# Performer attention and two feed-forward layers on one core: which queue positions the splits and sums take, and which engine adds the weight sums

## Chip, cores and metric

One core of one Trainium2 chip runs the whole program. The metric is the device time of one execution in microseconds (us); lower is better.

## What is computed

```python
def reference(**kwargs):
    ...
    attn_out = _attn_ref(**attn_kwargs)          # random-feature attention: 4 batches, 8 heads, 576 positions, 64 wide, 128 features
    x = np.ascontiguousarray(attn_out.transpose(0, 2, 1, 3)).reshape(B * S, H * D)   # 2304 x 512
    x = _moe_ref(x=x, **moe_kwargs)              # h = x @ w_in; (h * clip(h + 3, 0, 6) / 6) @ w_out, d_ff = 2048
    return _moe2_ref(x=x, **moe2_kwargs)         # h = x @ w_in; (h * sigmoid(1.702 h)) @ w_out
```

## The kernel before

All matrix products run in a split form: an fp32 operand becomes a high part (a ScalarE copy that rounds) and a low part (a VectorE subtract), and three products hi·hi, hi·lo, lo·hi are accumulated. Of each batch's 576 positions 512 form a block; the 64 left over of all four batches form one block of 256.

The first layer (to 578 us) goes over units (n, c): batch n, chunk c of 16 chunks of d_ff. `emit_h` multiplies a chunk (L501) and makes its gated, split activation (L512, L513, L517, L518; the last two are put into `gate`); `emit_o`, two units later, multiplies it with the output weights (L551). In between, a callback `side()`, called at two places of each, issues the attention of the next batch in small steps and, at every second call, one entry of the list `late`. `late` prepares the second layer's weights while batches 1 to 3 run: `convert_1` and `convert_2` rebuild them (GpSimd L195, VectorE L202), then `sums(u, n)` with n from 0 to 7 for each of 8 pairs of chunks u. `put_sums` copies a quarter pair with ScalarE (L218), subtracts with GpSimd (L219) and stores the result; `add_sums` (L231 to L234) replaces the quarters by sums and differences in place, four adds of 128x256 for each of the two weights.

The second layer multiplies 2x2 blocks with 7 products instead of 8, so it needs sums of blocks of x, of weights and of gated activations. It treats two batches at once, p = 0 and p = 1. `x_ops` makes the 14 split operands of x for one pair in 16 steps: twice (q = 0, 1) a load and seven parts, each a ScalarE copy (L637) and a VectorE subtract (L638), four of them with a GpSimd sum (L625 to L631). `h_pair` (L846) is called for u = 0 to 7 and gives the gated activations `gt[u, e]`; `o_pair` then runs the products 1, 7, 6, 5, 2, 3, 4, each over u = 0 to 7. I call one such u of one product a turn: 56 turns, 12 matmuls each (L965). For each turn `halves` splits one quarter of g into a ring of three `gs` buffers (ScalarE L939, VectorE L940), and `total` may add quarters in place on GpSimd for a later product (op 7 L955, op 6 L957, op 5 L959, op 4 L961). After each turn a callback `side()` issues steps of `x_ops` for the next pair, spread evenly.

Nothing here fixes the final order: the program is recorded in this order, and a scheduler then sets each engine's queue from data dependences, its own costs and the ties it is given. `tc.issue_after(ins)`, wrapped in `behind`, ties every instruction of a block behind `ins` if it is on the same engine; it is an order in the queue, not a wait. The queues are in order: an instruction that waits holds all behind it on its engine.

Of the kernel before, what the change touches and what calls it, by code (L numbers as in the profile page):

```python
# [1 line left out]

# [6 lines left out]
F32 = mybir.dt.float32  # L9
# [6 lines left out]
ALU = mybir.AluOpType  # L16
# [6 lines left out]
def performer_moe_kernel(  # L23
# [13 lines left out]
    nc = tc.nc  # L37
# [22 lines left out]
    PREP = 9  # L60
# [28 lines left out]
            return acc.tile(shape, F32, tag="acc", name="acc")  # L89
        return psp.tile(shape, F32, tag="ps", name="ps")  # L90

    def behind(i):
        return nullcontext() if i is None else tc.issue_after(i.ins)


    qkv = {}
# [130 lines left out]
    def add_sums(u, k):  # L227
        w0, w1 = whole[2 * u][:, k], whole[2 * u + 1][:, k]
        a11, a22 = w0[:, 0], w1[:, 1]
        a12, a21 = (w0[:, 1], w1[:, 0]) if k == 0 else (w1[:, 0], w0[:, 1])  # L230
        nc.vector.tensor_tensor(out=a22, in0=a21, in1=a22, op=ALU.add)  # L231
        nc.vector.tensor_tensor(out=a21, in0=a11, in1=a21, op=ALU.subtract)  # L232
        nc.vector.tensor_tensor(out=a11, in0=a22, in1=a11, op=ALU.subtract)
        nc.vector.tensor_tensor(out=a12, in0=a12, in1=a11, op=ALU.subtract)  # L234

    def sums(u, n):

# [516 lines left out]
    def side():  # L754
        pace[1] += 1
        if pace[1] % 2:
            late_at("side", 1)
            return
        while todo and (pace[0] - len(todo)) * 4 * NC < pace[0] * pace[1]:
            todo.pop()()  # L760
# [31 lines left out]
    for u in range(len(units) + LAG):  # L792
        while fetches and fetches[0][0] <= u + AHEAD:
            fetch_w(0, *fetches.pop(0)[1:])
        if u < len(units):
            n, c = units[u]
            if c == 0 and n + 1 < B:
                xblk[n + 1] = new_x(n + 1)
                steps = att_steps(Att(n + 1, xblk[n + 1], xl, n == 0))
                todo = steps[::-1]  # L800
                pace[:] = len(todo), 0
            if (n, c) == (B - 2, NC - 1):
                while todo:
                    todo.pop()()
                actx.close()
                lp = ctx.enter_context(
                    tc.tile_pool(name="lp", bufs=1, side="right", reuse_waits="tile")
                )
                xblk[B] = new_x(B)
                for kk in range(NK):  # L810
                    split_x(xl, xblk[B], kk)
            if n > 0:
                before_chunk(n, c)
            emit_h(n, c, side)
            if n == 0:
                convert_next(2, min(c + 2, NC), *(att.feat[H - 1] if c == 0 else ()))
            if n == B - 1 and c >= PREP:
                if c == PREP:
                    assert n_late[0] == len(late), (n_late, len(late))
                    prep = x_ops(0, wp, "w")  # L820
                    n_prep = len(prep)
                for _ in range(-(-n_prep // (NC - PREP))):
                    if prep:
                        prep.pop(0)()
            if c == NC - 1:
                while todo:
                    todo.pop()()
        if u >= LAG:
            emit_o(*units[u - LAG], side)
# [6 lines left out]
    def h_pair(p, u, first_split):  # L836

        psum, tag, oth, otag = (acc, "acc", psp, "ps") if u % 2 else (psp, "ps", acc, "acc")
        w = {}

        def product(op, kind, j, ps, first):
            s = w[kind][:, j].rearrange("p s (q f) -> p s q f", q=2)
            m = 0
            for q in range(2):
                for wi, xi in ((0, 0), (0, 1), (1, 0)):
                    nc.tensor.matmul(  # L846
                        out=ps,
                        lhsT=s[:, wi, q, :],
                        rhs=xop[q, op][:, xi],
                        start=(first and m == 0),  # L850
                        stop=(m == 5),
                        skip_group_check=not first,
                    )
                    m += 1

        def rest(e, ps):
            kinds = "ab"[e]
            m = 0
            for j in range(2):
                s = w[kinds][:, j].rearrange("p s (q f) -> p s q f", q=2)  # L860
                for q in range(2):
                    for wi, xi in ((0, 0), (0, 1), (1, 0)):
                        nc.tensor.matmul(  # L863
                            out=ps[:, e, :],
                            lhsT=s[:, wi, q, :],
                            rhs=xblk[B][:, xi, 2 * j + q, :],
                            start=(m == 0),
                            stop=(m == 11),
                        )
                        m += 1  # L870

        def bank():
            return psum.tile([P, SM], F32, tag=tag, name="h")

        def temp(pool, tag, name):
            return pool.tile([P, SM], F32, tag=tag, bufs=3, name=name)

        def add(out, a, b):
            nc.vector.tensor_tensor(out=out, in0=a, in1=b, op=ALU.add)  # L879

        def gated(i, src, eng):

            if i % 2 == 0 and (u, i // 2) not in gt:
                gt[u, i // 2] = l1.tile([P, 2, SM], F32, tag=f"g{2 * u + i // 2}", name="g")
            g = gt[u, i // 2][:, i % 2]
            nc.scalar.activation(out=g, in_=src, func=AF.Sigmoid, scale=1.702)  # L886
            eng.tensor_tensor(out=g, in0=g, in1=src, op=ALU.mult)  # L887

        last = p == B // 2 - 1
        w["a"] = next_item()  # L890
        b1, b6 = bank(), bank()
        product(1, "a", 0, b1, True)
        p1 = temp(gp, "ga", "p1")
        nc.scalar.copy(p1, b1)
        w["d"] = next_item()
        product(6, "d", 0, b6, True)
        u2 = temp(gp, "ga", "u2")
        add(u2, p1, b6)
        product(2, "a", 1, b1, False)
        gated(0, b1, nc.vector)  # L900
        if last:
            pl = oth.tile([P, 2, B * SL], F32, tag=otag, name="hl")
            rest(0, pl)
        w["c"] = next_item()
        b5, b7 = bank(), bank()
        product(5, "c", 1, b5, True)
        t = temp(gp, "ga", "t")
        add(t, u2, b5)
        product(7, "c", 0, b7, True)
        c22 = temp(lp, "gs", "c22")  # L910
        add(c22, t, b7)
        product(3, "d", 1, b5, False)
        c12 = temp(lp, "gs", "c12")
        add(c12, u2, b5)
        w["b"] = next_item()
        gated(2, c12, nc.gpsimd)
        gated(3, c22, nc.gpsimd)
        first_split()
        product(4, "b", 1, b7, False)
        c21 = temp(lp, "gs", "c21")  # L920
        add(c21, u2, b7)
        gated(1, c21, nc.gpsimd)
        if last:
            rest(1, pl)
            if u % 2 == 0:
                pool, tag = ((l1, "xr"), (xp_, "xl"), (l1, "gl"), (l1, "xr"))[u // 2]
                gl[u // 2] = pool.tile([P, 2, 2, B * SL], F32, tag=tag, bufs=2 if tag == "xr" else 1, name="gl")
            g = gl[u // 2][:, u % 2]
            nc.scalar.activation(out=g, in_=pl, func=AF.Sigmoid, scale=1.702)
            nc.vector.tensor_tensor(out=g, in0=g, in1=pl, op=ALU.mult)  # L930
# [2 lines left out]
    gl = {}  # L933

    ready = []

    def halves(pool, N, g):
        s = pool.tile([P, 2, N], F32R, tag="gs", bufs=3, name="gs")
        nc.scalar.copy(s[:, 0], g)  # L939
        nc.vector.tensor_tensor(out=s[:, 1], in0=g, in1=s[:, 0].bitcast(F32), op=ALU.subtract)  # L940
        return s

    def o_pair(p, side):
# [6 lines left out]

        def total(op, u):
            b11, b12, b21, b22 = quarters(u)
            add = nc.gpsimd.tensor_tensor
            if op == 7:
                add(out=b12, in0=b22, in1=b12, op=ALU.subtract)  # L955
            elif op == 6:
                add(out=b11, in0=b12, in1=b11, op=ALU.add)  # L957
            elif op == 5:
                add(out=b12, in0=b22, in1=b11, op=ALU.subtract)  # L959
            elif op == 4:  # L960
                add(out=b21, in0=b21, in1=b11, op=ALU.subtract)  # L961

        def rows(s, w, out, d, start, stop, fresh):
            for m, (wi, gi) in enumerate(((0, 0), (1, 0), (0, 1))):
# [8 lines left out]

        def product(op, ps, first):
            src = {1: 0, 7: 1, 6: 0, 5: 1, 2: 2, 3: 3, 4: 2}[op]
            ahead = {1: 7, 7: 6, 6: 5, 3: 4}.get(op)
            more = last and op in (2, 3, 4)
            for u in range(NC // 2):
                if u % 2 == 0:
# [88 lines left out]
    for p in range(B // 2):  # L1068
# [4 lines left out]
        if p + 1 < B // 2:  # L1073
            prep = x_ops(p + 1, l1, "xr") + [left_x]

        turn = [0, len(prep)]

        def side():
            turn[0] += 1
            while prep and (turn[0] - 6) * turn[1] > (turn[1] - len(prep)) * 48:  # L1080
                prep.pop(0)()

        o_pair(p, side)
        gt.clear()
# [58 lines left out]
```

## Time and profile before

| | before |
|---|---|
| median of 3 runs | 965.95 us (965.52 to 967.58) |
| the profiled execution | 966.03 us |
| its span, first to last instruction | 964.2 us |
| TensorE (PE) matmul busy | 922.5 us, 96% |
| VectorE (DVE) busy | 659.7 us, 68% |
| ScalarE (ACT) busy | 481.2 us, 50% |
| GpSimd (POOL) busy | 361.1 us, 37% |

The stages lie at 0 to 578 us (attention and first layer; the weights of the second are prepared from 200 to 500), 578 to 653 (`h_pair`, p = 0), 653 to 742 (`o_pair`, p = 0), 742 to 852 (`h_pair`, p = 1) and 852 to the end (`o_pair`, p = 1). A matmul's end is modelled, so a busy TensorE may still be short of its fastest pace; idle time of another engine costs nothing by itself. The granted TensorE clock is 1.00 throughout.

### The profile page before, as it was taken

To read this page: it belongs to the slowest core of one execution; us is meant where nothing else is said; L and a number is where in the kernel's file an instruction comes from. 1 tells how busy PE (TensorE), PEld (TensorE's weight loads), DVE (VectorE), ACT (ScalarE), POOL (GpSimd) and SP (SyncE) were. 2 spreads that over 40 slices of the span, in tenths; PEclk is the share of its full clock that TensorE was granted. 3 is DMA by queue.
4 is the path that set the end of the run, shared out by engine and by line. 5 is a ranking of instruction groups with operands and counts; after the bars stand their busy time and mean duration, and the time that the engine had idled before them with its cause. 6 is when DMAs were issued, how large, how long until landed. Compare 5 with 4: busy or idle time off the path is not lost.

```text
span 964.2 us, 16360 instructions
## 1 busy us (share of the span) xinstructions
PE 922.5 (96%) x6238; PEld 785.4 (81%) x6238; DVE 659.7 (68%) x1010; ACT 481.2 (50%) x977; POOL 361.1 (37%) x271
## 2 busy tenths in 40 slices
PE   8899999999999999999999999997799999999997
PEld 6777767778778777878888888886799888889997
DVE  7888889599686877847876244448976443378743
ACT  5887676566654665536544234334444232243443
POOL 0112222055352424425444005758822254364400
PEclk9999999999999999999999999999999999999999
DMA  6667778889777867756684237765567545555572
GB/s 195 226 233 247 243 255 267 294 293 351 263 269 283 311 244 277 249 206 240 241 292 166 93 134 257 232 206 189 158 178 237 181 169 175 168 176 165 173 259 88
DMA packets 71133, 214.06 MB, mean 222 GB/s; under 512 B 7056, under 2 KB 12816, under 8 KB 71056
## 3 DMA queue, kind: packets, MB, share of 16 engines
q1 hardware_dynamic: 70896, 212.77, 65.6%
q8 instruction: 49, 0.80, 0.3%
q10 hardware_dynamic: 160, 0.26, 0.1%
q14 instruction: 28, 0.23, 0.1%
HBM read 157.43 MB, written 55.57 MB: 221 GB/s over the span
## 4 chain that ended last, share of the span: by engine, by line
PE 48%; DVE 12%; ACT 3%; issue 2%; DMA 2%; POOL 1%; SPq 0%; DVEq 0%; POOLq 0%
PE o L965 16%; PE h L846 16%; PE o L551 6%; PE ps L501 5%; DVE gs L940 2%; PE hl L863 2%; DVE xo L638 2%; DMA xr<-xs 2%; DVE w L202 1%; DVE gs L518 1%; DVE w L231 1%; POOL w L195 1%; DVE ga L513 1%; DVE w L232 1%; PE ps L256 1%
## 5 line engine op out<-in xcount | busy, mean ns | idle before, releaser
L965 PE MATMUL o<-wss,gs 128*128 128x256 f32 x1536 | 190.9, 284 | 13.5 <-DVE gs L940 13.4
L965 PEld LDWEIGHTS o<-wss,gs 128*128 128x128 f32 x1536 | 186.3, 191 | 18.4 <-DVE gs L940 17.7
L501 PE MATMUL ps<-x,wss 128*128 128x512 f32 x768 | 194.0, 397 | 5.2 <-DVE ga L513 1.5
L501 PEld LDWEIGHTS ps<-x,wss 128*128 128x128 f32 x768 | 139.3, 188 | 38.0 <-ACT wss L205 3.0
L195 POOL TENSOR_TENSOR w<-w,wpow 128x512 f32<-128x512 f32 x64 | 78.2, 1241 | 235.8 <-DVE wpow L190 137.7
L846 PE MATMUL h<-xo,wss 128*128 128x512 f32 x672 | 160.6, 393 | 0.0
L940 DVE TENSOR_TENSOR gs<-g,gs 128x512 fp32r<-128x512 f32 x112 | 114.7, 1047 | 45.8 <-ACT gs L939 45.2
L846 PEld LDWEIGHTS h<-xo,wss 128*128 128x128 f32 x672 | 124.1, 188 | 26.4 <-issue 0.2
L219 POOL TENSOR_TENSOR wsn<-w,wsn 128x512 fp32r<-128x512 f32 x64 | 91.0, 1436 | 69.7 <-ACT wsn L218 63.4
L939 ACT CAST gs<-g 128x512 fp32r<-128x512 f32 x112 | 69.4, 620 | 95.4 <-PE o L965 90.1
L551 PE MATMUL o<-gs,wsh 128*128 128x512 f32 (+1 forms) x480 | 111.8, 377 | 1.2 <-DVE ob L580 1.0
L551 PE MATMUL o<-gs,wss 128*128 128x512 f32 (+1 forms) x480 | 109.6, 374 | 2.4 <-ACT gs L517 2.4
L887 POOL TENSOR_TENSOR g<-g,c 128x512 f32<-128x512 f32 x48 | 64.1, 1336 | 101.4 <-ACT g L886 100.9
L551 PEld LDWEIGHTS o<-gs,wss 128*128 128x128 f32 x480 | 81.7, 188 | 17.5 <-ACT gs L517 3.4
L551 PEld LDWEIGHTS o<-gs,wsh 128*128 128x128 f32 x480 | 81.7, 188 | 17.4 <-DVE ob L580 1.2
L513 DVE SCALAR_TENSOR_TENSOR ga<-ga,ps 128x512 f32<-128x512 f32 (+1 forms) x80 | 49.8, 627 | 59.4 <-ACT ga L512 59.0
L512 ACT ACTIVATE ga<-ps,three 128x512 f32<-128x512 f32 (+1 forms) x80 | 51.7, 653 | 67.9 <-PE ps L501 67.9
L264 ACT ACTIVATE e<-ps,mx 128x128 f32<-128x128 f32 x220 | 62.8, 394 | 31.7 <-DVE mx L262 31.5
L202 DVE TENSOR_TENSOR w<-w,wtop 128x512 f32<-128x512 f32 x64 | 68.1, 1073 | 12.5 <-POOL w L195 12.0
L518 DVE TENSOR_TENSOR gs<-ga,gs 128x512 fp32r<-128x512 f32 (+1 forms) x80 | 63.3, 802 | 13.3 <-ACT gs L517 11.9
L886 ACT ACTIVATE g<-c 128x512 f32<-128x512 f32 x48 | 30.3, 632 | 78.8 <-DVE c L879 78.8
L517 ACT CAST gs<-ga 128x512 fp32r<-128x512 f32 (+1 forms) x80 | 45.7, 581 | 30.9 <-DVE ga L513 30.7
(154 smaller groups left out, 1257.4 us busy)
## 6 DMA issues: line engine op xcount, KB each, us to landing
wss<-left SPq DMA_DIRECT2D x64, 512.0 KB, 3.7
wss<-ws0i SPq DMA_DIRECT2D x48, 512.0 KB, 4.8
wraw<-in_w_in_dram SPq DMA_DIRECT2D x32, 512.0 KB, 4.6
wraw<-in_w_out_dram SPq DMA_DIRECT2D x32, 512.0 KB, 5.9
left<-wsn SPq DMA_DIRECT2D x32, 512.0 KB, 4.8
wss<-ws0o SPq DMA_DIRECT2D x24, 512.0 KB, 4.9
ws0i<-wss SPq DMA_DIRECT2D x16, 512.0 KB, 3.1
wss<-sumsa SPq DMA_DIRECT2D x16, 512.0 KB, 3.2
```

What stands on the lines that cost most here:

```text
L195: nc.gpsimd.tensor_tensor(out=w[:, cols], in0=w[:, cols], in1=q[:, cols], op=ALU.mult)
L202: nc.vector.tensor_tensor(out=wj, in0=wj, in1=a[:, j * DM:(j + 1) * DM], op=ALU.add)
L219: nc.gpsimd.tensor_tensor(out=s[:, :, 1], in0=t, in1=s[:, :, 0].bitcast(F32), op=ALU.subtract)
L264: act = nc.scalar.activation(out=e[:, r, :], in_=ps[:, r, :], func=AF.Exp, bias=mx[:, r:r + 1])
L501: nc.tensor.matmul(out=ps, lhsT=w[:, wi, kk, :], rhs=x[:, xi, kk, :], start=(m == 0), stop=(m == 3 * NK - 1),)
L518: gate[1] = nc.vector.tensor_tensor(out=s[:, 1, :], in0=g, in1=s[:, 0, :].bitcast(F32), op=ALU.subtract)
L551: nc.tensor.matmul(out=ps[:, e, :], lhsT=w[:, wi, cols], rhs=s[:, gi, :], start=(c == 0 and m == 0 and per == 1), stop=(c == NC - 1 and m ...
L846: nc.tensor.matmul(out=ps, lhsT=s[:, wi, q, :], rhs=xop[q, op][:, xi], start=(first and m == 0), stop=(m == 5), skip_group_check=not first,)
L887: eng.tensor_tensor(out=g, in0=g, in1=src, op=ALU.mult)
L939: nc.scalar.copy(s[:, 0], g)
L940: nc.vector.tensor_tensor(out=s[:, 1], in0=g, in1=s[:, 0].bitcast(F32), op=ALU.subtract)
L965: nc.tensor.matmul(out=out, lhsT=s[:, gi, d * P:(d + 1) * P], rhs=w[:, wi, :], start=(start and m == 0), stop=(stop and m == 2), skip_grou ...
```

## The change

Five edits. `behind` takes several instructions. The adds of `add_sums` go from VectorE to GpSimd. In the first layer, the `late` entries that `side()` issues are tied behind `gate`, and the 16 `x_ops` steps of the first pair are issued by `side()`, one at every fourth call and tied too, instead of three per chunk. In `h_pair` the sum of op 7 is made on the spot, and `o_pair` makes the sums of ops 6, 5 and 4 in the phases of products 1, 6 and 2. In `o_pair`, the steps of `x_ops` are issued at the turns listed in `PLACES`, tied behind the newest split and sum.

```diff
-    def behind(i):
-        return nullcontext() if i is None else tc.issue_after(i.ins)
+    def behind(*ins):
+        stack = ExitStack()
+        for i in ins:
+            if i is not None:
+                stack.enter_context(tc.issue_after(i.ins))
+        return stack
...
-        nc.vector.tensor_tensor(out=a22, in0=a21, in1=a22, op=ALU.add)
-        nc.vector.tensor_tensor(out=a21, in0=a11, in1=a21, op=ALU.subtract)
-        nc.vector.tensor_tensor(out=a11, in0=a22, in1=a11, op=ALU.subtract)
-        nc.vector.tensor_tensor(out=a12, in0=a12, in1=a11, op=ALU.subtract)
+        nc.gpsimd.tensor_tensor(out=a22, in0=a21, in1=a22, op=ALU.add)
+        nc.gpsimd.tensor_tensor(out=a21, in0=a11, in1=a21, op=ALU.subtract)
+        nc.gpsimd.tensor_tensor(out=a11, in0=a22, in1=a11, op=ALU.subtract)
+        nc.gpsimd.tensor_tensor(out=a12, in0=a12, in1=a11, op=ALU.subtract)
...
         if pace[1] % 2:
-            late_at("side", 1)
+            with behind(*gate):
+                late_at("side", 1)
+                if prep and pace[1] % 4 == 1:
+                    prep.pop(0)()
             return
...
-            if n == B - 1 and c >= PREP:
-                if c == PREP:
-                    assert n_late[0] == len(late), (n_late, len(late))
-                    prep = x_ops(0, wp, "w")
-                    n_prep = len(prep)
-                for _ in range(-(-n_prep // (NC - PREP))):
-                    if prep:
-                        prep.pop(0)()
+            if (n, c) == (B - 1, PREP):
+                assert n_late[0] == len(late)
+                prep = x_ops(0, wp, "w")
...
         gated(1, c21, nc.gpsimd)
+        g = gt[u, 1]
+        nc.gpsimd.tensor_tensor(out=g[:, 0], in0=g[:, 1], in1=g[:, 0], op=ALU.subtract)
...
+    PLACES = (4, 10, 12, 14, 16, 26, 27, 28, 29, 30, 42, 44, 46, 48, 50, 52, 54)
+    split_ins = [None, None, None]
...
-        nc.scalar.copy(s[:, 0], g)
-        nc.vector.tensor_tensor(out=s[:, 1], in0=g, in1=s[:, 0].bitcast(F32), op=ALU.subtract)
+        split_ins[0] = nc.scalar.copy(s[:, 0], g)
+        split_ins[1] = nc.vector.tensor_tensor(
+            out=s[:, 1], in0=g, in1=s[:, 0].bitcast(F32), op=ALU.subtract
+        )
...
-            ahead = {1: 7, 7: 6, 6: 5, 3: 4}.get(op)
+            ahead = {1: 6, 6: 5, 2: 4}.get(op)
...
-        turn = [0, len(prep)]
+        turn = [0]
 
         def side():
             turn[0] += 1
-            while prep and (turn[0] - 6) * turn[1] > (turn[1] - len(prep)) * 48:
-                prep.pop(0)()
+            if prep and turn[0] in PLACES:
+                with behind(*split_ins):
+                    prep.pop(0)()
```

`total` keeps ops 6, 5 and 4 as a table (all now one line, L967) and stores its instruction in `split_ins[2]`. Lines after L92 shift: VectorE's split of g is L940 before and L947 now, its split of x L638 and L642, the sums of x L625 to L631 and L629 to L635.

What the scheduler makes of it is shown at three places, with the tile numbers that the build gives. The first is VectorE in the middle of the weight stretch (`w` are weights, `ga` and `gs` the activation and its split, `mx` a row maximum of the attention, `thi` and `tlo` a split of its input). Before:

```order
L231 TENSOR_TENSOR w_3207<-w_3207 128x256
L232 TENSOR_TENSOR w_3207<-w_3193,w_3207 128x256
L233 TENSOR_TENSOR w_3193<-w_3207,w_3193 128x256
L234 TENSOR_TENSOR w_3193<-w_3193 128x256
L513 SCALAR_TENSOR_TENSOR ga_3365<-ga_3365,ps_3348 128x512
L518 TENSOR_TENSOR gs_3368<-ga_3365,gs_3368 128x512
L231 TENSOR_TENSOR w_3207<-w_3193,w_3207 128x256
L232 TENSOR_TENSOR w_3193<-w_3193 128x256
L262 TENSOR_REDUCE mx_3427<-ps_3419 128x4
L233 TENSOR_TENSOR w_3193<-w_3207,w_3193 128x256
L234 TENSOR_TENSOR w_3207<-w_3207,w_3193 128x256
L313 CAST thi_3791<-qk_3391 128x512
```

Now:

```order
L517 SCALAR_TENSOR_TENSOR ga_3365<-ga_3365,ps_3348 128x512
L522 TENSOR_TENSOR gs_3368<-ga_3365,gs_3368 128x512
L266 TENSOR_REDUCE mx_3427<-ps_3419 128x4
L317 CAST thi_3791<-qk_3391 128x512
L266 TENSOR_REDUCE mx_3440<-ps_3433 128x4
L318 TENSOR_TENSOR tlo_3792<-qk_3391,thi_3791 128x512
L517 SCALAR_TENSOR_TENSOR ga_3467<-ga_3467,ps_3450 128x512
```

The eight adds of this pair of chunks have left the queue; the rest stands as it stood. They are now on GpSimd, between the subtracts of `put_sums`:

```order
L223 TENSOR_TENSOR wsn_3355<-w_3207,wsn_3355 128x2x256
L235 TENSOR_TENSOR w_3207<-w_3207 128x256
L236 TENSOR_TENSOR w_3207<-w_3193,w_3207 128x256
L237 TENSOR_TENSOR w_3193<-w_3207,w_3193 128x256
L238 TENSOR_TENSOR w_3193<-w_3193 128x256
L223 TENSOR_TENSOR wsn_3405<-w_3193,wsn_3405 128x2x256
L223 TENSOR_TENSOR wsn_3457<-w_3207,wsn_3457 128x2x256
L235 TENSOR_TENSOR w_3207<-w_3193,w_3207 128x256
L236 TENSOR_TENSOR w_3193<-w_3193 128x256
L237 TENSOR_TENSOR w_3193<-w_3207,w_3193 128x256
L238 TENSOR_TENSOR w_3207<-w_3207,w_3193 128x256
```

Before, only the L219 rows of `put_sums` stood there, one behind the other.

The second place is GpSimd from the last `h_pair` of p = 0 into `o_pair` (`g` gated activations, `c` unsplit ones, `xr` raw blocks of x for p = 1). Before:

```order
L957 TENSOR_TENSOR g_6675<-g_6708,g_6675 128x512
L627 TENSOR_TENSOR xr_7149<-xr_7151,xr_7149 128x512
L887 TENSOR_TENSOR g_7012<-g_7012,c12_7008 128x512
L631 TENSOR_TENSOR xr_7149<-xr_7149 128x512
L629 TENSOR_TENSOR xr_7151<-xr_7151,xr_7149 128x512
L955 TENSOR_TENSOR g_7012<-g_7012 128x512
L957 TENSOR_TENSOR g_6751<-g_6784,g_6751 128x512
L887 TENSOR_TENSOR g_6979<-g_6979,c21_7032 128x512
L957 TENSOR_TENSOR g_6827<-g_6860,g_6827 128x512
L957 TENSOR_TENSOR g_6903<-g_6936,g_6903 128x512
L957 TENSOR_TENSOR g_6979<-g_7012,g_6979 128x512
L959 TENSOR_TENSOR g_6480<-g_6480,g_6447 128x512
```

Now:

```order
L967 TENSOR_TENSOR g_6678<-g_6711,g_6678 128x512
L889 TENSOR_TENSOR g_7019<-g_7019,c12_7015 128x512
L926 TENSOR_TENSOR g_7019<-g_7019 128x512
L889 TENSOR_TENSOR g_6986<-g_6986,c21_7039 128x512
L967 TENSOR_TENSOR g_6755<-g_6788,g_6755 128x512
L967 TENSOR_TENSOR g_6832<-g_6865,g_6832 128x512
L967 TENSOR_TENSOR g_6909<-g_6942,g_6909 128x512
L967 TENSOR_TENSOR g_6986<-g_7019,g_6986 128x512
L629 TENSOR_TENSOR xr_7107<-xr_7107 128x512
L967 TENSOR_TENSOR g_6480<-g_6480,g_6447 128x512
L967 TENSOR_TENSOR g_6557<-g_6557,g_6524 128x512
L631 TENSOR_TENSOR xr_7105<-xr_7107,xr_7105 128x512
```

The sums of op 6 (`g_6751`, `g_6827` and so on) stood behind turns of product 1 already, and the sums of op 7 (the rows that read and write one `g` tile, such as `g_7012`) inside `h_pair`; that has not moved. Three sums of x that stood ahead of them (`xr_7149`, `xr_7151`) are gone from here, and the first of the next ones now stands behind all eight of op 6.

The third is VectorE over the same turns. Before:

```order
L940 TENSOR_TENSOR gs_7081<-g_6675,gs_7081 128x512
L879 TENSOR_TENSOR c12_7008<-u2_6971,h_6984 128x512
L638 TENSOR_TENSOR xo_7193<-xr_7149,xo_7193 128x512 x2
L638 TENSOR_TENSOR xo_7193<-xr_7151,xo_7193 128x512 x2
L879 TENSOR_TENSOR c21_7032<-u2_6971,h_6985 128x512
L940 TENSOR_TENSOR gs_7099<-g_6751,gs_7099 128x512
L638 TENSOR_TENSOR xo_7410<-xr_7149,xo_7410 128x512
L940 TENSOR_TENSOR gs_7115<-g_6827,gs_7115 128x512
L940 TENSOR_TENSOR gs_7133<-g_6903,gs_7133 128x512
L638 TENSOR_TENSOR xo_7504<-xr_7149,xo_7504 128x512
L940 TENSOR_TENSOR gs_7153<-g_6979,gs_7153 128x512
L638 TENSOR_TENSOR xo_7448<-xr_7151,xo_7448 128x512
```

Now:

```order
L881 TENSOR_TENSOR c12_7015<-u2_6978,h_6991 128x512
L881 TENSOR_TENSOR c21_7039<-u2_6978,h_6992 128x512
L947 TENSOR_TENSOR gs_7111<-g_6755,gs_7111 128x512
L947 TENSOR_TENSOR gs_7127<-g_6832,gs_7127 128x512
L947 TENSOR_TENSOR gs_7145<-g_6909,gs_7145 128x512
L947 TENSOR_TENSOR gs_7161<-g_6986,gs_7161 128x512
L947 TENSOR_TENSOR gs_7185<-g_6480,gs_7185 128x512
L947 TENSOR_TENSOR gs_7200<-g_6557,gs_7200 128x512
L642 TENSOR_TENSOR xo_7215<-xr_7105,xo_7215 128x512
L947 TENSOR_TENSOR gs_7220<-g_6634,gs_7220 128x512
L947 TENSOR_TENSOR gs_7235<-g_6711,gs_7235 128x512
L642 TENSOR_TENSOR xo_7215<-xr_7105,xo_7215 128x512
```

Before, four splits of x stood ahead of `c21`, and others between the splits of g (`gs`); eleven stood ahead of the first turn of product 6. Now four do, one after every second turn from turn 10 on.

## Rows read from the trace of the kernel before

**Rows 1.** Engines by stretch: busy us and count of PE, PEld, DVE, ACT, POOL; clock; DMA.
```profile
200.00:500.00 300.00, 290.40 (x1936) 236.44 (x1936) 230.35 (x370) 167.97 (x356) 130.86 (x97) 1.00 0.76 269
500.00:578.00 78.00, 77.32 (x447) 67.62 (x446) 35.52 (x51) 25.56 (x50) 12.50 (x8) 1.00 0.42 142
653.00:742.00 89.00, 77.15 (x606) 74.03 (x605) 76.24 (x73) 41.41 (x70) 52.04 (x32) 1.00 0.62 186
```

**Rows 2.** Waits of PE, 653 to 742 us: total us, times, longest us.
```profile
PE o L965 <- DVE gs L940: 11.8, 7, 2.5
```

**Rows 3.** Timeline of PE in `o_pair`: start us, us, line, tiles, shape, count, idle before.
```profile
664.07 1.70 PE L965 MATMUL o<-wss,gs 128*128 128x256 f32 x12 [2.03 <-DVE gs L940]
...
692.93 48.81 PE L965 MATMUL o<-wss,gs 128*128 128x256 f32 x396 [1.37 <-DVE gs L940]
```

**Rows 4.** Timeline of DVE in `o_pair`, same columns.
```profile
657.16 5.18 DVE L638 TENSOR_TENSOR xo<-xr,xo 128x512 fp32r<-128x512 f32 x4
...
665.63 3.44 DVE L940 TENSOR_TENSOR gs<-g,gs 128x512 fp32r<-128x512 f32 x2
...
691.12 8.05 DVE L940 TENSOR_TENSOR gs<-g,gs 128x512 fp32r<-128x512 f32 x6
...
710.01 0.69 DVE L940 TENSOR_TENSOR gs<-g,gs 128x512 fp32r<-128x512 f32 x1 [0.75 <-ACT gs L939]
...
716.87 1.27 DVE L1007 TENSOR_TENSOR ob<-ob,o 128x512 f32<-128x512 f32 x2
...
719.99 11.12 DVE L940 TENSOR_TENSOR gs<-g,gs 128x512 fp32r<-128x512 f32 x9
```

**Rows 5.** Timeline of POOL in `o_pair`, same columns.
```profile
656.47 1.31 POOL L957 TENSOR_TENSOR g<-g 128x512 f32<-128x512 f32 x1 [0.63 <-DVE gs L940]
...
692.29 1.73 POOL L959 TENSOR_TENSOR g<-g 128x512 f32<-128x512 f32 x1
...
717.02 1.29 POOL L961 TENSOR_TENSOR g<-g 128x512 f32<-128x512 f32 x1 [0.63 <-DVE gs L940]
...
720.88 8.49 POOL L961 TENSOR_TENSOR g<-g 128x512 f32<-128x512 f32 x5 [0.63 <-DVE gs L940]
```

**Rows 6.** Waits of PE, 200 to 500 us.
```profile
PE ps L256 <- DVE ga L513: 2.5, 3, 1.2
PE ps L375 <- ACT e L264: 1.9, 3, 1.3
PE ps L501 <- DVE ga L513: 1.5, 4, 0.6
PE ps L256 <- DVE llo L314: 1.3, 1, 1.3
```

**Rows 7.** Groups of DVE by shape, 200 to 500 us: busy us, mean ns, idle before.
```profile
L518 DVE TENSOR_TENSOR gs<-ga,gs 128x512 fp32r<-128x512 f32 x38 | 35.3, 932 | 10.6 <-ACT gs L517 9.5 <-PE ps L256 0.7
...
L231 DVE TENSOR_TENSOR w<-w 128x256 f32<-128x256 f32 x16 | 18.9, 1184 | 1.7 <-POOL wsn L219 1.6
L232 DVE TENSOR_TENSOR w<-w 128x256 f32<-128x256 f32 x16 | 14.5, 907 | 0.3
...
L233 DVE TENSOR_TENSOR w<-w 128x256 f32<-128x256 f32 x16 | 9.9, 617 | 0.3
L234 DVE TENSOR_TENSOR w<-w 128x256 f32<-128x256 f32 x16 | 7.8, 490 | 0.4
```

**Rows 8.** Groups of POOL by shape, 200 to 500 us.
```profile
L219 POOL TENSOR_TENSOR wsn<-w,wsn 128x512 fp32r<-128x512 f32 x64 | 91.0, 1436 | 69.7 <-ACT wsn L218 63.4 <-DVE mx L262 3.1 <-DVE x L246 3.1
...
L587 POOL TENSOR_TENSOR xl<-xl,xl 128x256 fp32r<-128x256 f32 x4 | 3.3, 852 | 20.7 <-ACT xl L586 20.7
```

**Rows 9.** Timeline of DVE and PE at one stop in the weight stretch.
```profile
276.01 1.50 DVE L231 TENSOR_TENSOR w<-w 128x256 f32<-128x256 f32 x1 [0.42 <-POOL wsn L219]
...
280.51 0.39 PE L256 MATMUL ps<-bd_hi,thi 128*128 128x256 f32 x1 [0.60 <-DVE ga L513]
```

**Rows 10.** The chain that ended last, in order of time, in `o_pair`: start us, us, what.
```profile
670.85 3.80 DMA xr<-xs
```

More of the change, by code (lines that the diff above doesn't have):

```diff
@@ L1 @@
-from contextlib import ExitStack, nullcontext
+from contextlib import ExitStack
 import concourse.bass as bass
@@ L952, in total @@
             b11, b12, b21, b22 = quarters(u)
[L953 to L961, printed above, removed]
+            out, in0, in1, add = {
+                6: (b11, b12, b11, ALU.add),
+                5: (b12, b22, b11, ALU.subtract),
+                4: (b21, b21, b11, ALU.subtract),
+            }[op]
+            split_ins[2] = nc.gpsimd.tensor_tensor(out=out, in0=in0, in1=in1, op=add)
         def rows(s, w, out, d, start, stop, fresh):
```

## Prediction

> **What bounds the kernel now.** I read the engines by stretch first. TensorE is idle 9.6 of 300 us while the weights are prepared, 0.7 of 78 after that, and 11.9 of 89 in the first `o_pair` [rows 1]. So two stretches can give time back.
>
> In `o_pair` all of TensorE's waits, 11.8 us in seven pieces, are for VectorE's split of g [rows 2]; they lie between 664 and 693, and from 692.93 on TensorE runs 48.8 us without one [rows 3]. VectorE's timeline shows why. From 657.16 to 692.8 it never stops: the first splits of x take 1.30 us each, two splits of g 1.72 each [rows 4]. When GpSimd has nothing to do the same split takes 0.69, at 710.01 [rows 4]. From 656.47 to the op at 692.29 GpSimd works almost without a pause [rows 5]. When both work, each goes at 1.70: five sums in 8.49 us [rows 5] beside VectorE's nine splits in 11.12 [rows 4]. An add that reads PSUM is not slowed: 1.27 for two beside a sum of 1.29 [rows 4, 5]. So the cost is a pair: one GpSimd op and one VectorE op with both inputs in SBUF, together 1.70 us.
>
> In the weight stretch the waits are short and many. The three largest that name a VectorE output directly are 2.5, 1.5 and 1.3, and 1.9 more comes through the row maximum and ScalarE's exponential [rows 6]. One of them shows the pattern: the adds of the weights start at 276.01, the first takes 1.50 instead of some 0.43, the gated activation stands behind them, and TensorE stops for 0.60 at 280.51 [rows 9].
>
> **The change part by part.**
>
> *Sums of op 7, 6 and 4 moved in the code.* In the queue they stand where they stood (the second place above). Nothing, both ways.
>
> *Splits of x in `o_pair`, first part.* I count up to the first turn of product 6, which TensorE started at 692.9. Before, VectorE ran 25 ops from 657.16 to 692.8: 13 splits of g, 11 of x, one add from PSUM; GpSimd ran 20 in that time. By pairs that is 20 x 1.70 + 5 x 0.69 = 37.5 us against 35.7 measured, so the rule holds to 5%. Now VectorE has 18 ops (7 fewer splits of x), and GpSimd 17 up to the last sum of op 5: 17 x 1.70 + 1 x 0.69 = 29.6 us. That is 6.1 us earlier. The first of these splits can start only when TensorE frees a buffer, so I take **5.0**. Bounds: 0 if the pairs take the time all the same, 11.8 if every wait goes [rows 2]. After that turn TensorE sets the pace in both.
>
> *Splits of x, second part.* Ten of the 14 parts now come in products 5, 3 and 4. In product 5 GpSimd is nearly idle and four splits at 0.69 fit beside five turns; nothing. Behind the eight sums of op 4 GpSimd now goes straight on to two sums of x, and a split of x joins. Before, those eight sums were just hidden: nine splits in 11.12 us beside them [rows 4, 5], and no wait of TensorE [rows 3]. Three more pairs instead of single splits cost 3 x (1.70 - 0.69) = 3.0, and the split of x 0.69: 3.7 us on VectorE. The ring of three `gs` buffers can hide some of it or all. I take **-2.0** between 0 and -3.7.
>
> *The load for q = 1* is issued when the last part of q = 0 is done, and takes 3.8 us [rows 10]. ScalarE's copy for the next part waits for it, with a copy of g behind. By the queue it is due three turns later, 4.3 us at the 1.44 us that one split follows the other in the undisturbed part, 0.69 and an idle 0.75 [rows 4]. Nothing; bound 0.6. *The small block of x* now splits in product 4 on ScalarE and on GpSimd (four at 0.85 [rows 8]); its first reader comes after that product. Nothing, bound 1.
>
> *The x steps of p = 0* move to later units. VectorE is busy 35.5 of 78 us there and TensorE idle 0.7 [rows 1]. Their second load now stands behind the last weight loads on SyncE's queue; it has some 30 us. Nothing.
>
> *Weight adds.* On VectorE the 64 adds took 18.9 + 14.5 + 9.9 + 7.8 = 51.1 us of its 230.4 [rows 7, 1]. These go. On GpSimd 64 adds of 128x256 take 64 x 0.852 = 54.5 us [rows 8], so its 130.9 busy us become 185 of 300: it still has room. What is given back: the splits L518 already take 932 ns on average instead of 690 [rows 7], and more GpSimd ops meet more of them. Of the 5.3 us of direct waits [rows 6] I take **3.0**. Bounds: 7.2 for all of rows 6; below, a loss, told under the last rival. *The tie* puts ScalarE's copies of `put_sums` behind the copy of the activation: ScalarE is busy 168 of 300 [rows 1], nothing by itself.
>
> The second `o_pair` and the two `h_pair` stretches have the same queue order as before; nothing.
>
> **Sum**: 966.03 (the profiled execution; its span 964.2 and 1.8 around it) - 5.0 + 2.0 - 3.0 = **960.0**. The median of the runs, 965.95, is 0.1 lower than that execution, which changes nothing here.
>
> **A rule against the trace.** Rows 4 and 5 give 1.70 us for a pair whose members take 0.69 and 1.30 alone. The Trainium skill, SBUF — State Buffer, "Who interferes with whom", says that a VectorE instruction with two SBUF inputs and a GpSimd instruction that reads SBUF exclude each other fully, the later one blocking until the first is done. By that a pair would cost 1.99 and the new first part 17 x 1.99 + 0.69 = 34.5 us, a gain of 1.2 instead of 6.1. The trace disagrees on the size: by the same rule the old stretch would have taken 43 us, and it took 35.7; it agrees that ops reading PSUM are spared.
>
> **The rivals.**
>
> *GpSimd falls behind and pairs less.* A sum of op 5 must wait for a split of the turn before it; if it lags, VectorE runs alone at 0.69 and TensorE's waits all go: -11.8, no loss in the second part, -3.0 for the weights: 951.2. For it: TensorE alone needs only 12 x 1.44 = 17 us for these turns. Against: nothing holds the sums of op 6 and of x back.
>
> *The gain only changes place.* The second part costs its full 3.7 against the first's 5.0, and the adds cost as many pairs in the weight stretch as they free: 966.03 - 1.3 = 964.7. For it: GpSimd gets 54.5 us more, and VectorE's two-input ops are a large part of its time [rows 7]. Against: the adds themselves ran at 1184 and 907 ns where 430 would do.
>
> *Slower: GpSimd becomes the chain of the weights.* The third copy of `put_sums` must wait for four adds. Each is 0.852 on GpSimd [rows 8] against 0.49 for the least disturbed on VectorE [rows 7], and they stand behind subtracts of 1.44 [rows 8]: a chain grows by 4 x 0.36 = 1.4 us, 16 of them by 23 us. ScalarE's queue waits with that copy, and the next activation behind it. If a third reaches TensorE, +7.7 - 3.0 = +4.7: 970.7. It decides from the point where these copies wait longer than the two units by which the output products lag. For it: GpSimd already waited 63.4 us for these copies, so the two work hand in hand [rows 8]. Against: a step comes only at every second callback, so there are microseconds between them. The Trainium skill, GPSIMD Engine Reference, "Performance versus the Vector engine", calls GpSimd the wrong choice for plain elementwise work, 1.96 times slower on an add; 852 against 490 ns agrees.
>
> **How the numbers follow.** Forecast (about 956 to 963) 0.50; the first rival (948 to 956) 0.20; the second (963 to 968) 0.18; slower 0.12. The range 952 to 967 leaves out the lower half of the first rival and the slower one. About 0.2%, 1.9 us, can be told from no change: faster holds the forecast, the first rival and a small part of the second, 0.74; same 0.14; slower 0.12.
>
> **What would show it.** In `o_pair`, p = 0: TensorE's waits for the split of g fall from 11.8 to about 6, the first wait (2.03) is gone, and a new one of 1 to 3 us stands in product 3; splits of x after product 2 take 0.69 unless a sum of x runs. In the weight stretch: VectorE's busy time falls from 230 to near 195, GpSimd's rises to 185 or more, and TensorE's idle falls by some 3 us. Wrong it is if ScalarE's copies of `put_sums` wait for GpSimd by microseconds, if VectorE's splits there get slower than 932 ns by as much as the adds freed, or if the waits in `o_pair` stay.

## The result and the profile after

The changed kernel took **949.5 us** (949.34 to 950.15, 4 runs) beside 965.74 of the kernel before (4 runs): ratio 0.9832, 95% interval 0.9815 to 0.9849. The forecast of 960.0 had the direction, but the time is 2.5 us below the lower end of the range. The profiled execution took 949.58; its span, 947.8, is 16.4 shorter than before.

Where the time went is seen by cutting both traces at the same rows of TensorE. The first cut is a group of 16 attention matmuls (`ps<-v,e`) that starts at 203.53 before and at 202.89 after, ahead of the first weight add (206.62 before). The second is the first matmul of `o_pair`, at 652.86 before and at 640.03 after. Between the two, before and after, with the columns of [rows 1] (length of the stretch, then TensorE's busy time and number of matmuls):

```profile
203.53:652.86 449.33, 439.05 (x2690) 362.21 (x2690) 295.55 (x464) 219.35 (x447) 185.89 (x139) 1.00 0.70 243
202.89:640.03 437.14, 436.70 (x2690) 362.72 (x2689) 245.82 (x400) 219.04 (x443) 231.90 (x198) 1.00 0.73 249
```

So **12.2 us** come from the stretch in which the weights are prepared. The 0.6 us at the first cut are not the change's: in seven runs with its first layer that row starts anywhere from 202.89 to 204.09. From the second cut to the end of p = 0's products it is 88.9 us before (to 692.93 + 48.81) and 85.4 after (to 714.88 + 10.59): **3.4 us**. The rest is the same to 0.3 us.

Engines by stretch after, to set beside [rows 1]; the last line is the first `o_pair`:

```profile
200.00:500.00 300.00, 299.56 (x2002) 246.68 (x2001) 190.88 (x311) 171.13 (x361) 181.65 (x161) 1.00 0.79 278
500.00:578.00 78.00, 78.00 (x433) 67.72 (x432) 30.29 (x53) 28.68 (x53) 13.51 (x9) 1.00 0.46 154
640.00:725.00 85.00, 77.37 (x603) 73.80 (x602) 74.77 (x72) 40.18 (x68) 53.06 (x34) 1.00 0.63 193
```

TensorE idles 0.44 us of 300 instead of 9.6, and does 66 matmuls more in the same time. VectorE fell by 39.5 us and GpSimd rose by 50.8, both as forecast (to some 195, to 185).

TensorE's timeline in the first `o_pair` after; [rows 3] has that of before:

```profile
640.03 2.20 PE L971 MATMUL o<-wss,gs 128*128 128x256 f32 x17
645.33 13.30 PE L971 MATMUL o<-wss,gs 128*128 128x256 f32 x103
660.32 3.39 PE L971 MATMUL o<-wss,gs 128*128 128x256 f32 x24 [1.68 <-DVE gs L947]
665.38 3.38 PE L971 MATMUL o<-wss,gs 128*128 128x256 f32 x24 [1.68 <-DVE gs L947]
670.45 3.13 PE L971 MATMUL o<-wss,gs 128*128 128x256 f32 x24 [1.68 <-DVE gs L947]
674.45 38.76 PE L971 MATMUL o<-wss,gs 128*128 128x256 f32 x312 [0.87 <-DVE gs L947]
714.88 10.59 PE L971 MATMUL o<-wss,gs 128*128 128x256 f32 x84 [1.67 <-DVE gs L947]
```

The wait of 2.03 is gone, four are left in products 7 and 6, one is new in product 3: 7.6 us in all instead of 11.8 [rows 2]. Each is a split of x that stands among splits of g while GpSimd runs sums. VectorE's and GpSimd's timelines show the pair of the prediction twice, and a free split in between:

```profile
656.82 1.77 DVE L642 TENSOR_TENSOR xo<-xr,xo 128x512 fp32r<-128x512 f32 x1
658.51 3.44 DVE L947 TENSOR_TENSOR gs<-g,gs 128x512 fp32r<-128x512 f32 x2
688.56 0.69 DVE L642 TENSOR_TENSOR xo<-xr,xo 128x512 fp32r<-128x512 f32 x1
711.38 1.78 DVE L642 TENSOR_TENSOR xo<-xr,xo 128x512 fp32r<-128x512 f32 x1
```

```profile
656.30 1.74 POOL L629 TENSOR_TENSOR xr<-xr 128x512 f32<-128x512 f32 x1
658.00 3.40 POOL L967 TENSOR_TENSOR g<-g 128x512 f32<-128x512 f32 x2
710.86 1.74 POOL L629 TENSOR_TENSOR xr<-xr 128x512 f32<-128x512 f32 x1
```

### The profile page after: what moved, and what is told of

Read it like the earlier page. It is cut to its first block, busy times and chain, and to the rows that moved or that the text cites. A ratio compares the mean times of both kernels' runs of the same rounds, so it can differ in the third digit from the quotient of the medians.

```text
span 947.8 us, 16356 instructions
## 1 busy us (share of the span) xinstructions
PE 920.7 (97%) x6238; PEld 786.5 (83%) x6238; DVE 609.9 (64%) x946; ACT 481.9 (51%) x977; POOL 411.5 (43%) x335
## 4 chain that ended last, share of the span: by engine, by line
PE 76%; DVE 15%; ACT 4%; issue 2%; DMA 2%; POOL 1%; SPq 0%; POOLq 0%; DVEq 0%; ACTq 0%
PE ps L505 17%; PE h L848 16%; PE o L555 16%; PE o L971 16%; DVE gs L947 4%; PE ps L260 3%; DVE w L206 3%; PE hl L865 2%; PE ps L393 1%; POOL w L199 1%; PE ps L357 1%; DVE mx L266 1%; DVE gs L522 1%; ACT wtop L182 1%; DVE wtop L190 1%
## 5 line engine op out<-in xcount | busy, mean ns | idle before, releaser
L947 DVE TENSOR_TENSOR gs<-g,gs 128x512 fp32r<-128x512 f32 x112 | 118.7, 1085 | 38.8 <-ACT gs L946 38.8
L967 POOL TENSOR_TENSOR g<-g 128x512 f32<-128x512 f32 x48 | 75.0, 1582 | 50.2 <-DVE gs L947 50.2
```

The source lines that it names most:

```text
L947: split_ins[1] = nc.vector.tensor_tensor(out=s[:, 1], in0=g, in1=s[:, 0].bitcast(F32), op=ALU.subtract)
L967: split_ins[2] = nc.gpsimd.tensor_tensor(out=out, in0=in0, in1=in1, op=add)
```

## Experiments

All medians are of runs beside the kernel before on the same chip. "Weights" is the time in the profiled run between the two cuts above; "pairs" is the time from the second cut to the first matmul of the second `o_pair`.

| kernel | us | ratio to before | weights | pairs |
|---|---|---|---|---|
| before | 965.2 to 966.3 | 1 | 449.3 | 195.8 |
| the change | 949.5 | 0.983 [0.982, 0.985] | 437.1 | 192.2 |
| e1 change, adds on VectorE | 952.1 | 0.987 [0.986, 0.989] | 439.1 | 192.6 |
| e2 before, adds on GpSimd | 957.9 | 0.992 [0.991, 0.994] | 442.0 | 195.7 |
| e3 before, tie of the late steps | 955.4 | 0.990 [0.988, 0.991] | 439.1 | 195.6 |
| e4 change, old spread in `o_pair` | 953.2 | 0.988 [0.986, 0.989] | 436.9 | 195.8 |
| e5 change, old place of x for p = 0 | 950.1 | 0.984 [0.982, 0.986] | 436.8 | 192.8 |
| e6 before, tie on ScalarE alone | 957.0 | 0.990 [0.989, 0.992] | 440.4 | 195.6 |
| e7 before, tie on VectorE alone | 963.9 | 0.997 [0.996, 0.998] | 444.7 | 195.6 |
| e9 change, sums on VectorE | 937.8 | 0.971 [0.970, 0.972] | 437.3 | 182.9 |
| e10 change, other places | 946.4 | 0.979 [0.978, 0.981] | 436.9 | 188.9 |
| e11 e9 with the old spread, untied | 944.6 | 0.977 [0.975, 0.979] | 436.9 | 189.4 |
| e12 before, sums on VectorE | 958.3 | 0.992 [0.990, 0.994] | 448.8 | 190.3 |
| e13 change, even spread, tied | 951.8 | 0.985 [0.983, 0.987] | 436.7 | 193.9 |
| e14 e9 with even spread, tied | 936.3 | 0.969 [0.968, 0.971] | 437.5 | 181.8 |

### What gave the 12.2 us of the weight stretch

**e1**, the adds back on VectorE:

```diff
-        nc.gpsimd.tensor_tensor(out=a22, in0=a21, in1=a22, op=ALU.add)
+        nc.vector.tensor_tensor(out=a22, in0=a21, in1=a22, op=ALU.add)
...
```

> The changed kernel with the 64 weight adds back on VectorE, all else as changed. Theory A (VectorE's relief by the adds gives the 12 us of the weight stretch): about 961 to 962 us, TensorE's busy time in 200:500 falls from 299.6 back to some 290, VectorE's there rises from 191 to 230 or more. Theory B (the tie of the late steps behind the activation's copy gives them): the time stays near 950, TensorE's busy time there near 299, though VectorE's rises by the 39 us. Theory C (both are needed, each alone gives a part): 954 to 958.

952.1, between theories B and C; the weight stretch is 1.9 us longer than with the change, and TensorE is busy 297.5 us of 200:500 (99.26 + 100.00 + 98.27 by hundreds), nearer to B's 299 than to A's 290. **e2** is the kernel before with the opposite edit in its four lines.

> The kernel before with only the 64 weight adds moved to GpSimd. Theory A (the adds): 953 to 954 us, that is all of the 12 us of the weight stretch; o_pair p = 0 stays at 89 us. Theory B (the tie): no gain, 965 to 966, or slower, up to 971, where ScalarE's copies of put_sums wait for GpSimd. Theory C (both): 958 to 962.

957.9, at the edge of C: alone the adds are worth 7.3 us. **e3**, the tie alone:

```diff
-            late_at("side", 1)
+            with behind(*gate):
+                late_at("side", 1)
```

> The kernel before with only the tie: a late step of the weights that is issued at every second callback stands in the queues behind the activation's copy and split. Theory A (the adds): 965 to 966 us, TensorE's busy time in 200:500 near 290. Theory B (the tie): 953 to 955, near 299. Theory C (both): 960 to 963.

955.4, theory B within half a us: the tie alone gives 9.8, with the adds still on VectorE. So the two remove in large part the same waits: 7.3 + 9.8 = 17.1 against about 12 for both (e4, whose `o_pair` is as long as before). TensorE's idle time between the two cuts says the same: 10.3 us before, 0.4 with the change, and here 4.0 in e2 and 2.5 in e3:

```profile
203.95:645.99 442.04, 438.06 (x2690) 362.56 (x2689) 255.58 (x400) 219.29 (x446) 237.40 (x203) 1.00 0.71 246
203.59:642.71 439.12, 436.63 (x2690) 362.99 (x2689) 291.30 (x464) 219.78 (x447) 184.91 (x139) 1.00 0.72 248
```

A place that the traces have in common shows how. Before, ScalarE and VectorE, and TensorE further on:

```profile
404.33 0.69 ACT L512 ACTIVATE ga<-ps,three 128x512 f32<-128x512 f32 x1 [1.65 <-PE ps L501]
405.48 0.62 ACT L218 CAST wsn<-w 128x512 fp32r<-128x512 f32 x1 [0.46 <-DMA sumsa<-wsn]
409.30 0.62 ACT L517 CAST gs<-ga 128x512 fp32r<-128x512 f32 x1 [2.60 <-DVE ga L513]
...
405.53 0.76 DVE L231 TENSOR_TENSOR w<-w 128x256 f32<-128x256 f32 x1
406.32 1.42 DVE L232 TENSOR_TENSOR w<-w 128x256 f32<-128x256 f32 x1
407.78 0.42 DVE L233 TENSOR_TENSOR w<-w 128x256 f32<-128x256 f32 x1
408.24 0.43 DVE L234 TENSOR_TENSOR w<-w 128x256 f32<-128x256 f32 x1
408.58 0.68 DVE L513 SCALAR_TENSOR_TENSOR ga<-ga,ps 128x512 f32<-128x512 f32 x1
...
410.56 1.53 DVE L231 TENSOR_TENSOR w<-w 128x256 f32<-128x256 f32 x1
412.13 1.40 DVE L232 TENSOR_TENSOR w<-w 128x256 f32<-128x256 f32 x1
413.46 0.68 DVE L262 TENSOR_REDUCE mx<-ps 128x4 f32<-128x512 f32 x1
...
415.36 0.65 PE L375 MATMUL ps<-ident,e 128*128 128x128 f32 x4 [1.27 <-ACT e L264]
```

The gate is two steps: ScalarE's activation, done at 405.02, and VectorE's multiply L513. The multiply stands behind four adds and starts 3.56 us later; ScalarE waits 2.60 for it. The next adds stand ahead of a row maximum, L262, and for the exponential that needs it TensorE waits 1.27. In e3:

```profile
399.05 0.69 ACT L516 ACTIVATE ga<-ps,three 128x512 f32<-128x512 f32 x1 [0.15 <-PE ps L505]
...
399.77 0.69 DVE L517 SCALAR_TENSOR_TENSOR ga<-ga,ps 128x512 f32<-128x512 f32 x1 [1.19 <-ACT ga L516]
400.37 0.88 DVE L235 TENSOR_TENSOR w<-w 128x256 f32<-128x256 f32 x1
```

The multiply starts 0.03 us after the activation, and the adds come behind it. **e6** and **e7** tie to one of the two instructions only:

```diff
-            late_at("side", 1)
+            with behind(gate[0]): late_at("side", 1)     # e6; e7: gate[1]
```

> The kernel before with a late step tied behind the copy of the activation on ScalarE alone: ScalarE's copies of put_sums can no longer stand ahead of it; VectorE's adds are not tied themselves (they follow the copies that read the same data). The full tie alone gave 9.8 us. Theory K (the copies on ScalarE's queue cost it): 955 to 957. Theory V (the adds on VectorE's queue, ahead of the gated activation and the row maximum, cost it): 963 to 966, unless the adds come later with the copies.

957.0. It would be wrong to read this as theory K's proof: at the place above e6 has the same order on VectorE as e3 (multiply at 399.59, adds from 400.19). Most likely the adds moved with the copies that read the same data; no run shows that apart.

> The kernel before with a late step tied behind the activation's split on VectorE alone: the weight adds there can no longer stand ahead of it; ScalarE's copies are untied. Theory V (the adds on VectorE's queue cost the waits): 955 to 958, as with the adds moved to GpSimd (957.9) or the full tie (955.4). Theory K (the copies on ScalarE): 963 to 966.

963.9 (961.5 to 964.8; the profiled execution is the fastest of seven), the number of theory K. But its rows at the same place are those of before with other times:

```profile
401.71 0.69 ACT L512 ACTIVATE ga<-ps,three 128x512 f32<-128x512 f32 x1 [1.64 <-PE ps L501]
...
402.92 0.76 DVE L231 TENSOR_TENSOR w<-w 128x256 f32<-128x256 f32 x1
...
405.95 0.68 DVE L513 SCALAR_TENSOR_TENSOR ga<-ga,ps 128x512 f32<-128x512 f32 x1
```

`gate` holds the split of the unit before, and behind that the adds stood anyway. Elsewhere the tie did something: the profiled execution idles 6.9 us between the cuts instead of 10.3. So e7 is no test of theory V; e2, which takes the adds off VectorE, is. At this place a late step before the change was pulled ahead of the next gate's multiply; the edits that take its adds from there gave 7.3 (e2), 8.9 (e6) and 9.8 (e3) of about 12 us. No run moves ScalarE's copies without moving the adds, so what the copies cost by themselves stays open. ScalarE's own waiting at its copies of `put_sums` is seen in their group, 200 to 578 us, the last columns being its idle time before them: before, in e2 and after.

```profile
L218 ACT CAST wsn<-w 128x512 fp32r<-128x512 f32 x63 | 38.2, 627 | 29.5 <-issue 14.5 <-DVE rden L415 3.5 <-DMA sumsc<-wsn 2.8
```

```profile
L218 ACT CAST wsn<-w 128x512 fp32r<-128x512 f32 x63 | 38.0, 623 | 57.6 <-POOL w L234 27.3 <-issue 15.6 <-POOL w L232 6.4
```

```profile
L222 ACT CAST wsn<-w 128x512 fp32r<-128x512 f32 x63 | 37.8, 626 | 24.5 <-issue 9.4 <-POOL w L238 9.0 <-DVE rden L419 3.5
```

With the adds on GpSimd and no tie, ScalarE waits 57.6 us at these copies, 33.7 of it for the adds: the chain that the slower rival named, and longer than the 23 us it gave. With the tie it falls to 24.5, 9.0 of it for the adds. But little of it reaches TensorE: of the 4.0 us that TensorE idles in e2, only a wait of 0.27 at 285.97 follows such a copy. Half, 1.95, are two stops of another kind: ScalarE's copies of x for p = 0, untied in e2 as before, wait for their load in front of an activation.

```profile
499.87 1.14 ACT L637 CAST xo<-xr 128x512 fp32r<-128x512 f32 x2 [6.43 <-DMA xr<-xs]
500.92 1.04 ACT L512 ACTIVATE ga<-ps,three 128x512 f32<-128x512 f32 x2
...
502.47 3.03 PE L501 MATMUL ps<-x,wss 128*128 128x512 f32 x12 [1.34 <-DVE ga L513]
520.37 3.03 PE L501 MATMUL ps<-x,wss 128*128 128x512 f32 x12 [0.61 <-DVE ga L513]
```

Another 1.48 stand at 315.82 and 317.01 behind VectorE's work for the attention, where the kernel before stops too (1.33 at 319.29). So, as far as idle time shows it, the 4.7 us that e4 gains over e2 by its ties (957.9 to 953.2) are in the main not the price of that chain.

**e5** puts the x steps of p = 0 back (three per unit, untied).

> The changed kernel with the x steps of p = 0 put back: three per unit, untied, instead of one at every fourth callback behind the activation's copy. Theory (they lie beside other work, as forecast): 949 to 950. Rival (ScalarE's copies of x wait for their load in front of activations, as the kernel before showed 9 us of such waits): 951 to 954.

950.1, its weight stretch the same to 0.3 us: nothing, as forecast. That holds while the late steps are tied; in e2, where they are not, the two stops of 1.95 us stand behind the x steps.

### What gave the 3.4 us of `o_pair`

**e4**, and **e13** with the tie kept:

```diff
-            if prep and turn[0] in PLACES:
-                with behind(*split_ins):
-                    prep.pop(0)()
+            while prep and (turn[0] - 6) * turn[1] > (turn[1] - len(prep)) * 48:
+                prep.pop(0)()                # e13: inside "with behind(*split_ins)"
```

> The changed kernel with the x steps of o_pair spread evenly and untied as before (the list of places undone). If the list of places gives what o_pair p = 0 gained (85.3 against 88.9 us): 953.1 us, the stretch back at 88.9 with seven or eight waits of TensorE for the split of g of about 1.7 each. Rival (o_pair gained because it starts from another state of the queues, after faster weights): 949.5, the stretch stays at 85.3. The weight stretch before it should not change in either case.

953.2, the pairs again 195.8: the stretch owes its gain to this edit alone, not to the earlier start. The waits were expected to be seven or eight; the trace shows five, 8.8 us in all, in a stretch as long as before's with seven and 11.8.

> The changed kernel with the x parts of o_pair at the even places of before (9, 12, 15, 18, 21, 23, ...), but tied behind the split of g as in the change. Theory L (the list gives the 3.7 us: in turns with a sum of g beside the split each part of x costs a wait of 1.68, wherever the queue has it): 952 to 955, six or more such waits. Theory T (the tie gives it, since it keeps parts of x from standing ahead of splits of g): 949 to 951.

951.8, between T and L: of the 3.7 us the tie gives 1.4 and the list 2.3 by the medians, 1.9 and 1.7 by "pairs", so about half each. It has six waits, four of them of 1.67 or 1.68, where a part of x meets the sums; one of these:

```profile
659.10 5.09 PE L971 MATMUL o<-wss,gs 128*128 128x256 f32 x36 [1.68 <-DVE gs L947]
```

**e10** puts no part of x into products 1, 7 and 6:

```diff
-    PLACES = (4, 10, 12, 14, 16, 26, 27, 28, 29, 30, 42, 44, 46, 48, 50, 52, 54)
+    PLACES = (4, 25, 26, 27, 28, 29, 31, 32, 33, 41, 42, 44, 46, 48, 50, 52, 54)
```

> The changed kernel with another list of places: no part of x in products 1, 7 and 6 (4, 25 to 29, 31 to 33, 41, 42, then 44 to 54 by twos). Theory P: in products 7 and 6 a split of g and a sum at 1.70 together just fill TensorE's turn of 1.69, each part of x there costs one wait of about 1.7; four of these waits (5.9 us) go and that in product 3 (1.67) stays or doubles: 942 to 946. Rival (the waits go where the parts go, in product 5 and 3): 948 to 951.

946.4, 0.4 beyond the poor end of P: the four waits go, one of 1.00 comes in product 5, and of product 3's 1.67 there are now 1.68 and 0.61. TensorE needs 38.69 us for the 295 matmuls from 645.97, 24.6 turns at 1.57. **e9** takes the sums themselves away from GpSimd:

```diff
-            split_ins[2] = nc.gpsimd.tensor_tensor(out=out, in0=in0, in1=in1, op=add)
+            split_ins[2] = nc.vector.tensor_tensor(out=out, in0=in0, in1=in1, op=add)
...
-            add = nc.gpsimd.tensor_tensor
+            add = (nc.vector if p else nc.gpsimd).tensor_tensor
```

> The changed kernel with the sums of g in o_pair, and those of x for the second pair, on VectorE instead of GpSimd. Theory P (a GpSimd sum costs VectorE's split 1.70 - 0.69 = 1.01 us; a sum done by VectorE itself costs 0.69 and slows nothing): in products 1 and 7 VectorE then has 27 ops x 0.69 = 18.6 us for 16 turns of 1.69 = 27 us, so TensorE's waits for the split of g go, 7.6 us in the first o_pair and 1.6 in the second: 940 to 942. Rival (VectorE has too many ops to issue in time, or an op that writes f32 from two SBUF tiles is slower than the split): waits of TensorE for the split stay, 947 to 953.

937.8, 2.2 better than theory P. VectorE's groups in the first `o_pair`, of the change and of e9 (busy us, mean ns, idle before):

```profile
L947 DVE TENSOR_TENSOR gs<-g,gs 128x512 fp32r<-128x512 f32 x49 | 57.0, 1197 | 8.3 <-ACT gs L946 8.3
L642 DVE TENSOR_TENSOR xo<-xr,xo 128x512 fp32r<-128x512 f32 x13 | 14.4, 1104 | 0.4 <-ACT xo L641 0.4
```

```profile
L947 DVE TENSOR_TENSOR gs<-g,gs 128x512 fp32r<-128x512 f32 x47 | 33.5, 727 | 8.1 <-ACT gs L946 8.0
L967 DVE TENSOR_TENSOR g<-g 128x512 f32<-128x512 f32 x21 | 15.2, 734 | 0.3
L642 DVE TENSOR_TENSOR xo<-xr,xo 128x512 fp32r<-128x512 f32 x12 | 8.2, 686 | 2.1 <-ACT xo L641 2.1
L629 DVE TENSOR_TENSOR xr<-xr 128x512 f32<-128x512 f32 x2 | 1.4, 684 | 0.0
```

The sums of x are four groups like the last (L629, L631, L633, L635). VectorE does 29 sums more, with three splits fewer on record, and is busy with all of these 8.9 us less (62.5 against 71.4). The Trainium skill, GPSIMD Engine Reference, "Performance versus the Vector engine", advises against GpSimd for plain elementwise work; here the time agrees, by 11.7 us. In the weight stretch the opposite move gained 7.3 us (e2): there the adds stood in front of work that TensorE needed.

**e11** (e9 with e4's spread) and **e12** (the kernel before with e9's edit) ask whether the places still matter then.

> The kernel with the sums on VectorE (937.8) and the x parts of o_pair spread evenly and untied as before. Theory P: the waits came from GpSimd's sums beside the splits; without them VectorE has room for a part of x in any turn, the list of places is worth nothing: 937 to 939. Rival (the list is worth what it was with the sums on GpSimd, 3.7 us): 941 to 943.

> The kernel before with only the sums of o_pair (of g, and of x for the second pair) on VectorE. Theory P: TensorE's waits for the split of g, 11.8 us in the first o_pair and 1.6 in the second, go, and some 2 to 3 us that its slow pace hides: 949 to 952, more than the list of places gave (3.7). Rival (without the list VectorE's extra ops keep half of the waits, or the first sum of x waits for its load at the head of VectorE's queue): 954 to 959.

944.6, beyond the rival's 943, and 958.3, within the rival's range. VectorE's and TensorE's timelines of e11 show the first and longest wait (e12 has its like, 2.16 at 663.91):

```profile
645.82 3.01 DVE L642 TENSOR_TENSOR xo<-xr,xo 128x512 fp32r<-128x512 f32 x3
648.75 1.78 DVE L631 TENSOR_TENSOR xr<-xr 128x512 f32<-128x512 f32 x1
650.45 0.68 DVE L642 TENSOR_TENSOR xo<-xr,xo 128x512 fp32r<-128x512 f32 x1
...
652.38 1.69 PE L971 MATMUL o<-wss,gs 128*128 128x256 f32 x12 [2.17 <-DVE gs L947]
```

Untied, three parts of x and a sum run in one burst that ends as TensorE already waits for a split of g. **e14** is e11 with the tie:

> The kernel with the sums on VectorE, the x parts at the even places of before, tied. Untied it took 944.6, with the list and tied 937.8. Theory T (untied parts are pulled forward into one burst ahead of the splits of g; with sums on VectorE the places themselves are worth nothing): 937 to 939. Theory L (the places count): 942 to 945.

936.3, just below theory T's 937, and the fastest kernel here: 3.1% below the kernel before, 1.4% below the change. TensorE runs 44 turns with no stop:

```profile
651.81 64.15 PE L971 MATMUL o<-wss,gs 128*128 128x256 f32 x528 [0.32 <-DVE gs L947]
```

## Why the prediction was wrong, step by step

- *Splits of x in `o_pair`, first part: -5.0.* Right. To the first turn of product 6 it was 40.1 us (652.86 to 692.93) and is 34.4 (640.03 to 674.45): -5.6. The 18 VectorE ops of the sum ran from 645.60 to that wait's end at 674.45, 28.9 us against the 29.6 forecast.
- *Second part: +2.0.* Right. 48.8 us from there before, 51.0 now (674.45 to 725.47): +2.2, with the wait in product 3 where it was named. The pair of 1.70 carried both sums. The gain of 1.2 under a pair of 1.99 was wrongly worked out: it takes a modelled new stretch (34.5) from a measured old one (35.7). On like terms, 43 to 34.5, it is 8.5, against 7.9 for the pair of 1.70 (37.5 to 29.6); so the gain does not decide between the two, and the rows of the pairs, 1.70 each, do.
- *Weight adds: -3.0, bound 7.2; the tie: "nothing by itself".* **This is the step that failed**, and it holds 9.2 of the 10.5 us of error: the two gave 12.2. First, I priced the tie by how busy ScalarE is (168 of 300), though the prediction's own example [rows 9] had the fault that the tie mends, adds ahead of the gate's multiply; a busy share says nothing about order. Alone it gave 9.8 us (e3). Second, I took 3.0 for the adds because of "what is given back". Alone they gave 7.3 (e2). The give-back was there, but small: the splits went from 932 ns [rows 7] to 1103 in e2 and 963 with the change, some 7 us in e2 for 51 us of adds that left VectorE. Third, the bound was too low. It was made from a list of waits, which leaves out the smaller ones and all time that TensorE lost while the profile calls it busy. Between the two cuts idle time fell by 9.8 us (10.28 to 0.44); the other 2.4 us of the 12.2 had counted as busy (439.05 to 436.70 for the same 2690 matmuls).
- *The load for q = 1, the small block, the x steps of p = 0, the second `o_pair`: nothing.* Borne out for the x steps (e5), given the tie; the stretch behind the first `o_pair` is unchanged. The first two were not tried apart.
- *Rivals.* "GpSimd falls behind" gave 951.2, near the time by luck: its way was another, for waits stayed in `o_pair` (7.6 us) and the weights gave four times its 3.0. "The gain only changes place" did not happen. The slower one's chain exists (e2, 33.7 us of waits on ScalarE) but shows 0.27 us of TensorE's idle time behind it, and the tie shortened it. So the sign that the prediction named for being wrong there, copies of `put_sums` that wait for GpSimd by microseconds, came true even with the change (9.0 us) and meant nothing.

## What to carry to other kernels

Price an order tie by what it moves out from in front of a stalled instruction, not by the share of time that the engine is busy; two edits against the same waits don't add up (17.1 for 12 here). Where two engines slow each other, add the times of a pair before giving work to the idle one: VectorE with GpSimd's sums on top was busy for less time than with GpSimd beside it (62.5 against 71.4 us). Steps that a scheduler may place freely need a tie as well as a place; without the tie the same even spread was 8.3 us slower with the sums on VectorE (e11, e14) and 1.4 slower with them on GpSimd (e4, e13).

## What the runs showed of the hardware that I had not expected

TensorE's busy time hides waiting. In turns where VectorE makes a pair per turn, 24 matmuls take 3.39 us with no idle shown inside (660.32 of the change); unhindered, 528 take 64.15, or 2.92 for 24. So e9 gained 9.3 us in "pairs", where the change shows only 7.6 us of waits for the split of g, and 3.5 from the first matmul of the second `o_pair` to the end (115.6 to 112.1), where it shows 1.6. The gain to expect from a stall is better counted from start to start of equal pieces of work than from idle time.
